# A third MLP pass moves to fifteen block products, with buffers and the instruction order rearranged to allow it

## The chip, the cores and the metric

The kernel runs on one core of a Trainium2 chip. The metric is the device time of one execution in microseconds (us). A core has five engines with an instruction queue each: PE (matrix products), DVE (vector), ACT (scalar functions and copies), POOL (vector work, slower) and SP (here it only issues transfers). Every engine runs its queue in order; an instruction that waits for a semaphore holds up all that stand behind it. Transfers (DMA) are issued from the queues of SP, ACT and POOL.

## The reference, cut to what matters

```python
# B, H, S, D = 4, 8, 768, 48; all float32; weights 384x1536 and 1536x384
k_n = k / (norm(k) + 1e-6)
for t in range(S):                      # a delta-rule recurrence per batch and head
    y[t]  = q[t] @ state
    v_old = k_n[t] @ state
    state = state + beta[t] * outer(k_n[t], v[t] - v_old)
x  = y as (B, S, H*D)                   # (4, 768, 384)
xn = (x - mean(x)) / sqrt(var(x) + 1e-6) * g_ln
out = x + maximum(xn @ w_ch1, 0) @ w_ch2
```

The weights arrive as 64-bit floats and are read as pairs of 32-bit words.

## The kernel before

**Chunks.** The sequence is cut into 12 chunks of 64 positions. All 32 recurrences (4 batches x 8 heads) run side by side. Within a chunk the recurrence is solved in closed form: the Gram matrix G of the chunk's keys, scaled by beta and the key norms, gives a unit triangular matrix whose inverse X turns values into updates u. With the state S before the chunk: u = X(v - K S), y = Q S + (masked Q K^T) u, and S grows by K^T u.

In the code: `products` builds G (`gram`, L834) and the query products (`queries`, L843); `recur(c)` (L1021) holds a chunk's steps: K S and Q S (L1033), u (L1088), the state's growth (L1105, read from raw keys in `kraws`), y (L1095), copies of y (L1133), layer norm (L1139 to L1155), and the turned, normalised activations `xnt` (by PE transposes for chunks 0 to 2, `LNPE`, by way of DRAM later).

**Inverses.** For chunk 0 `first_inverse` (L707) doubles the block size in five rounds; a round is a product E (L771), a predicated copy (DVE, L752 or L776), a product Z (L786), transposes (DVE, L735) and copies (ACT, L729). Ahead of it stand the transposes of raw keys (L628) and their copies out of PSUM (ACT, L633), the squares of the keys (ACT, L654), the norms' roots (ACT, L656) and G (L695, L743). For later chunks `rows_inverse` (L865) solves rows of blocks for many heads at once: 31 pairs of DVE instructions (L907, L914). Keys and queries come as blocks by `load_blocks` into a tile `tb[i]` and are turned there by DVE (`turned`, L799); key blocks alternate between `tb[0]` and `tb[2]`, issued on POOL's queue (L401).

**Weights.** Twelve pieces are fetched as words from ACT's queue (`fetch`) and turned into 32-bit floats by `convert`: ACT (L584, L592), DVE (L589), POOL (L602).

**MLP.** `mlp(c)` is one pass over the 256 rows of a chunk. In its plain form the first product takes 12 x 3 matmuls of 128x128 by 256 columns (L1407). From pass `FROM` on it runs as `fifteen(c)`: W1 and the activations are cut into 3x3 and 3x2 blocks, and 15 products of sums of blocks, each 4 matmuls of 128 columns (L1307), take the place of 18 block products. The sums of activations are made on POOL (`mix`, L1290), the results combined on ACT (L1325, L1334) and DVE (L1330), and the sums of W1 once, by `sums_of_w1` on POOL and DVE (L1265, L1267), half in place and half in new tiles. The second product is `seven(c)` from pass 1 on: 7 products instead of 8 (L1504), with combinations of hidden activations on POOL (L1491, L1529). Pass 0 uses the plain form (L1429).

**Order.** Every instruction group is a numbered step. `Line.emit` writes them out in the order of the string `ORDER`, which fixes each engine's queue; an assertion demands that a step's declared reads and writes (the key tuples) have gone before. The word `f` in `ORDER` puts in a filler: a product of zeros, 128x256, on PE (L1582). `due`, `cap`, `pr` and `t0` are arguments of the planner that made the string, and play no part when the program is built.

```python
FROM, LATER = 3, 6
kraws = [sb(f"kr{i}", [128, GH * DP]) for i in range(3)]
more = [t.rearrange("p h t -> p (h t)") for t in (qts[1], pts[1])] + [sb("w_more", [128, 2 * FB4])]
```

Of the kernel before, what the change touches and what calls it, by code (L numbers as in the profile page):

```python
# [16 lines left out]
C = 64  # L17
# [106 lines left out]
def act(n):  # L124
    return 0.17 + 0.83e-3 * n
# [6 lines left out]
47 9 6 257 8 48-49 10-11 13 1 32 26 23 14 0 12 65 7 66 60 39-43 256 45-46 44 61 55 74 53-54 52 58-59 327 56-57 63  # L132
405 408 64 37 21 5 17 30 71 35 73 69 75 238 79-80 82 85-86 96 89 88 36 29 15-16 20 4 18-19 90 33 97 87 91-92 3 93
98-99 83 100 94 84 101 81 106 104-105 103 76 38 27 95 102 124 22 125 118 126 239 119 24 77 108 70 107 109-110 215 78
226 127 111 122 121 112 129 72 246 123 240 128 213 133 25 134 120 f f 130 31 114 28 131-132 f f 135-137 141 115 2
142-143 222 139 138 140 147-150 216 145 230-231 146 144 157 151 116-117 214 159 153 152 158 209-210 163 250 154-155
161-162 160 156 211 164 113 401 403 314-316 412 260 325 67 313 326 265 410 259 262 68 264 263 266 261 413-414 328
407 409 212 f f 168 165 227 166-167 248 232 218 172-173 171 174 318 228 178 249 170 169 175-176 317 180-183 241 233
229 217 251 320 177 319 179 242 244 267 224 234 f 185 321 184 186 191 268-269 50 192 34 270-271 187 273 258 272 638
245 193 274-279 219 280 f f 197 243 322 370 329 323 188 195 330 189-190 331 194 196 247 369 332 363 650 652 399 199  # L140
198 200-201 205 333 204 364 202-203 206-207 334 208 335 f f f f 339 337 281-290 235 223 291-296 338 297-298 340 299
252 300-301 51 302-303 62 640 225 469 400 f 341-342 371 343-344 361-362 236-237 642 654 347 253 348 365 352 f f 435
434 402 324 404 336 411 304 474 477 406 476 475 307 305 767 309-310 312 308 311 306 437 436 345-346 353 372 349-351
354 220 373 367 221 374 f f f 438 355 359 439 360 366 440 415 357-358 356 478 577 575 254 578 581 479 368 255
480-482 418 416 473 484 643 641 637 644 656 649 655 639 653 768-769 771 773 772 770 766 419 576 375-376 579 614 420
580 583-584 379 377 582 388 381-382 421 485-503 422 504-509 378 510 423 511 645 587 615 585 616-617 387 588 591 424
586 592 428 427 426 595-596 425 417 380 651 589 429 441 599 618-619 442 774 512-523 394 430 433 431 590 383 432 393
443-444 385 389 445 593 524-526 390 657 527-528 448 446-447 384 529 600-602 646 908 449-450 391 397 395 1052 1054
1064 386 530 453 531 454 451-452 392 1066 603 647 604 658 620-621 594 458 455 605-606 597 607 659 456 532-533 459
534 460 457 461 465-466 464 467-468 463 462 598 622-623 608 396 535 483 398 1068 1065 536-539 629 540 630 541 631  # L150
542-543 632 544-547 633 609 778 775 805 624 610 625 806 910 912 763 907 911 764 914 901 648 913 660 909 900 662 1160
663-665 915 776 548 1056 1051 1057 1055 666 765 906 661 611 626 667-670 672 1162 550 549 551 903 552 628 627 673-674
902 905 1163 904 1165 1157 1167 613 811-812 807 777 809 817 810 818 675-677 815 808 816 823 821-822 824 813-814 1070
1069 829 832 830 833 1067 1053 678 779 679-690 553 691-701 554-558 838 819 702-704 634 705-706 564 707-711 559 827
839-840 562 561 560 563 828 820 780 841-842 848-849 843 781 712 1063 831 835 845 836 713 784 782 714 565 786 785 567
844 789 787 783 790 834 1058 825 850 715 788 568 826 794 791 566 569 795 716-717 796 792 718-719 793 720 855-856
851-852 865 916 853-854 801 797 570 866 846 873 867 837 802 799 804 574 572 571 800 573 803 798 917 721 1059 1526
847 1525 918 722-723 920 724 635 725-728 857 868 874-875 869 876 919 921 870 858 877 859-860 729-730 636 731-735
1347 1166 1348 1155-1156 1164 612 1168 736 1169 922-923 871 861 880-883 671 924 1071 1060 878-879 925 1061 1072
471-472 470 862 1528 1538 1170 1161 863-864 954 948 1073 927 891-893 956-957 884 894 872 926 895 962 896 1171 897  # L160
885 960 930-931 935 963 968 928 936 929 1540 1530 949 1075 951 950 739-740 1352 1062 1074 737-738 1077 1076
1078-1079 1172 886 969 961 932 937 741 1173 742 745-746 1080 958-959 743 974-975 744 887-888 955 980 953 933 952 752
# [78 lines left out]
2937-2938 2909 2939 2930 2940 2910 2964-2965 2954-2955 2941 2956 2942 2933 2957-2958 2966 2959 2943 2934 2967 2944  # L241
2960 2935 2968-2969 2971-2972 2945 2948 2946-2947 2970 2952 2951 2961 2981 2949-2950 2962 2953 2989 2982 2990-2992
2983 2963 2984 2993-2994 2973 2985-2986 2974-2976 2979-2980 2978 2995 2987 2996 2988 2997-3001 2977 3002 3007-3012
3003-3004 3013 3005 3014-3015 3006
"""


# [1482 lines left out]
```

## Time and profile before

| what | value |
|---|---|
| time, median of 3 runs | 529.24 us (527.1 to 530.44) |
| the profiled execution's own time | 530.82 us |
| its span, from first to last instruction | 529.1 us |
| PE busy | 496.1 us, 94% of the span |
| DVE busy | 358.6 us, 68% |
| POOL busy | 284.3 us, 54% |
| ACT busy | 207.2 us, 39% |
| first MLP product starts | 75.18 us |
| PE busy, 0 to 80 us | 58.0 us |

How to read the profile: all times are from one execution. A row of a timeline gives start, length, engine, line, output and inputs, shapes and count, and in brackets the idle time before it with what ended it. A float32 matmul leaves two records. Matmuls are pipelined, so the mean length of one record is longer than the step from one to the next; that step is what a product costs. "PEclk", the granted clock, is 1.00 at full speed. The chain that ended last is followed back from the last instruction, at each step to what released it.

### The profile page before, as it was taken

How to read it: one execution, taken by the hardware profiler on the slowest of the kernel's cores; microseconds unless marked ns; L12 is line 12 of the kernel's file. 1: busy time of each engine (PE TensorE's matmuls, PEld its weight loads, DVE VectorE, ACT ScalarE, POOL GpSimd, SP SyncE). 2: the span in 40 equal slices, each digit the busy share in tenths (PEclk: the TensorE clock that was granted, in tenths of full speed). 3: DMA queues.
4: the chain of work that ended last, by engine and by line, in shares of the span. 5: the costliest groups of instructions: out<-in, count | busy, mean ns of one | idle time of the engine just before them, and what ended most of it. 6: DMA issues, size and time to landing. Idle time of an engine off the chain costs nothing.

```text
span 529.1 us, 22717 instructions
## 1 busy us (share of the span) xinstructions
PE 496.1 (94%) x9938; PEld 451.6 (85%) x9938; DVE 358.6 (68%) x819; ACT 207.2 (39%) x451; POOL 284.3 (54%) x447
## 2 busy tenths in 40 slices
PE   5667988999999999989999999999999999999996
PEld 2455776767888889979999999999999999999996
DVE  2547778878997599986899954998837436354241
ACT  1786562542442334233261452353423424424130
POOL 7004485447245967767649437346374362554644
PEclk9588899999999999999999999999999999999999
DMA  9876759749543893159357267234343502102011
GB/s 178 200 161 122 211 89 233 118 121 164 101 69 81 178 156 55 35 147 191 60 120 135 48 184 126 45 85 75 97 100 71 117 4 60 34 33 59 1 32 30
DMA packets 181635, 54.56 MB, mean 103 GB/s; under 512 B 164888, under 2 KB 177312, under 8 KB 181536
## 3 DMA queue, kind: packets, MB, share of 16 engines
q1 hardware_dynamic: 168512, 40.10, 37.9%
q10 hardware_dynamic: 10816, 9.83, 6.7%
q0 software_dynamic: 2208, 3.17, 3.6%
q8 instruction: 78, 1.28, 1.0%
q14 instruction: 21, 0.17, 0.1%
HBM read 36.30 MB, written 16.78 MB: 100 GB/s over the span
## 4 chain that ended last, share of the span: by engine, by line
PE 85%; DVE 5%; issue 3%; DMA 2%; ACT 2%; SPq 1%; ACTq 0%; POOL 0%; DVEq 0%
PE f L1504 28%; PE f L1307 22%; PE f L1407 9%; PE two L819 3%; PE f L1429 3%; PE f L1582 2%; PE by L1033 2%; PE by L1095 2%; PE two L1088 2%; PE two L1033 2%; PE two L1105 2%; DVE xb L914 1%; DMA words<-in_moe_w_ch_dram 1%; SPq L401 1%; DMA kr<-in_k_dram 1%
## 5 line engine op out<-in xcount | busy, mean ns | idle before, releaser
L1504 PE MATMUL f<-w_sb,h_all 128*128 128x192 f32 x396 | 81.8, 329 | 0.0
L1491 POOL TENSOR_TENSOR h_all<-h_all 128x256 f32<-128x256 f32 x99 | 72.9, 753 | 14.9 <-DVE tmp L907 6.1
L1504 PE MATMUL f<-words,h_all 128*128 128x192 f32 x396 | 78.4, 330 | 0.1
L1330 DVE TENSOR_TENSOR h_all<-f,h_all 128x512 f32<-128x512 f32 x72 | 49.1, 686 | 33.3 <-PE f L1307 25.4
L1529 POOL TENSOR_TENSOR words<-h_all 128x128 f32<-128x128 f32 x66 | 31.2, 491 | 70.0 <-ACT h_all L1334 34.2
L1504 PEld LDWEIGHTS f<-w_sb,h_all 128*128 128x128 f32 x396 | 65.3, 190 | 1.1 <-POOL h_all L1491 0.2
L1504 PEld LDWEIGHTS f<-words,h_all 128*128 128x128 f32 x396 | 64.8, 190 | 1.4 <-issue 0.2
L914 DVE TENSOR_TENSOR xb<-xb,tmp 128x31 f32<-128x31 f32 (+19 forms) x139 | 58.8, 423 | 3.1
L907 DVE TENSOR_TENSOR tmp<-xb,gb 128x31 f32<-128x31 f32 (+19 forms) x139 | 53.0, 381 | 4.0 <-POOL xb L894 0.6
L1407 PE MATMUL f<-xnt,w_sb 128*128 128x256 f32 x216 | 52.6, 391 | 0.3 <-issue 0.3
L1325 ACT COPY h_all<-f 128x512 f32<-128x512 f32 x45 | 26.0, 586 | 58.8 <-PE f L1307 41.0
L401 POOL DMA_DIRECT2D tb<-in_k_dram x64 | 42.0, 660 | 13.0 <-DVE xb L914 7.4
L1334 ACT ACTIVATE h_all<-h_all 128x512 f32<-128x512 f32 x54 | 32.3, 625 | 36.2 <-DVE h_all L1330 36.0
L1407 PEld LDWEIGHTS f<-xnt,w_sb 128*128 128x128 f32 x216 | 40.4, 192 | 7.0 <-ACT h_all L1416 0.4
L1307 PE MATMUL f<-x_new,w_sb 128*128 128x128 f32 x288 | 39.8, 277 | 1.3 <-DVE h_all L1330 1.1
L1307 PE MATMUL f<-xnt,w_sb 128*128 128x128 f32 x288 | 40.7, 277 | 0.0
L1522 DVE TENSOR_TENSOR o<-f,x 128x192 f32<-128x192 f32 x33 | 11.6, 354 | 41.7 <-PE f L1504 24.9
L602 POOL TENSOR_TENSOR w_sb<-words 128x768 uint32<-128x768 uint32 (+1 forms) x11 | 15.0, 1365 | 43.3 <-DVE words L589 33.4
L1307 PEld LDWEIGHTS f<-x_new,w_sb 128*128 128x128 f32 x288 | 36.7, 192 | 1.7 <-issue 1.5
L1307 PEld LDWEIGHTS f<-xnt,w_sb 128*128 128x128 f32 x288 | 37.1, 191 | 0.3
L1133 ACT COPY x<-by 128x384 f32<-128x384 f32 x23 | 10.4, 481 | 53.2 <-POOL o L1522 36.3
L1416 ACT ACTIVATE h_all<-f 128x256 f32<-128x256 f32 x36 | 13.4, 383 | 35.1 <-PE f L1407 34.9
(252 smaller groups left out, 987.4 us busy)
## 6 DMA issues: line engine op xcount, KB each, us to landing
words<-in_moe_w_ch_dram ACTq DMA_DIRECT2D x20, 384.0 KB, 4.6
gd<-gsb SPq DMA_DIRECT2D x11, 512.0 KB, 3.9
v<-in_v_dram SPq DMA_DIRECT2D x24, 192.0 KB, 3.9
kr<-in_k_dram SPq DMA_DIRECT2D x46, 96.0 KB, 3.6
out_dram<-o SPq DMA_DIRECT2D x46, 96.0 KB, 2.3
xld<-xlt SPq DMA_DIRECT2D x9, 384.0 KB, 2.5
xnt<-xld SPq DMA_DIRECT2D x36, 96.0 KB, 3.0
tb<-in_q_dram SPq DMA_DIRECT2D x40, 64.0 KB, 2.9
```

The source lines that it names most:

```text
L401: add(eng, cost, lambda: QUEUE[eng].dma_start(out=out_, in_=in_), r, w, bulk=n * ns / 16e3, np=n, **kw)
L907: lambda j=j, n=n, w=w, t=t: nc.vector.tensor_tensor(out=t, in0=xv[:, 0:n, j : j + 1].to_broadcast([128, n, w]), in1=gv[:, j : j + 1, j + ...
L914: "DVE", dve(n * w), lambda t=t, rest=rest: nc.vector.tensor_tensor(out=rest, in0=rest, in1=t, op=ALU.subtract),
L1033: nc.tensor.matmul(dst[half(e), hp, j], src[drows(hp), (e if n else key_half(c, hp, e)) * GP + j], s_all[drows(hp), e, j], start=(n == 0 o ...
L1307: nc.tensor.matmul(wide(p[:, f : f + 128]), w[:, f : f + 128], r, start=start and i == 0, stop=True, skip_group_check=True)
L1325: add("ACT", act(512), lambda: nc.scalar.copy(o, p), pk, ok)
L1330: add("DVE", dve(512), lambda: nc.vector.tensor_tensor(out=o, in0=x, in1=y, op=op), [*xk_, *yk], ok)
L1334: add("ACT", act(512), lambda: nc.scalar.activation(o, o, ACTF.Relu, scale=scale), [], ok)
L1407: nc.tensor.matmul(p[:, 0:TOK], w1_sb[:, t, f * 128 : (f + 1) * 128], xnt[:, t], start=(t == 0), stop=(t == KC - 1))
L1491: add(eng, cost, lambda: e.tensor_tensor(out=out_, in0=x, in1=y, op=op), r, w, port=2 if eng == "Pool" else 1, pr=-2)
L1504: lambda f=f, t=start and f == order[0]: nc.tensor.matmul(p[:, 0:D2], lhs(f), rhs[:, f], start=t, stop=(f == order[-1]), skip_group_check=True
L1529: lambda f=f + i: e.tensor_tensor(out=s3[f], in0=one(0, 0)[0](f), in1=one(1, 0)[0](f), op=ALU.subtract),
```

## The change

`FROM` goes from 3 to 2, so the pass of chunk 2, until now plain, uses the fifteen products; 10 of 12 passes do. Its activations lie in another order (`LNPE`), so `fifteen` takes a second view for them. W1's sums must be ready a pass earlier, while the second tiles for q and P are still in use; they get two tiles of their own and `tb[2]`. To make room, raw keys have two buffers instead of three, and from chunk 4 on all key blocks go through `tb[0]`. Chunks 2 and 3 load raw keys into `tb[0]` and `tb[2]`.

Besides, a tiny square root of one column moves to the front of ACT's work (a key "act" makes copies and conversions follow it), `convert` of half a piece counts both halves' transfers as read, POOL's clearing of all of `tb[0]` becomes DVE's clearing of its padding, and the whole `ORDER` is new, with 30 fillers in place of 19.

```diff
-    FROM, LATER = 3, 6
+    FROM, LATER = 2, 6
...
-    kraws = [sb(f"kr{i}", [128, GH * DP]) for i in range(3)]
+    kraws = [sb(f"kr{i}", [128, GH * DP]) for i in range(2)]
...
-    more = [t.rearrange("p h t -> p (h t)") for t in (qts[1], pts[1])] + [sb("w_more", [128, 2 * FB4])]
+    more = [sb(f"w_more{i}", [128, 2 * FB4]) for i in range(2)] + [tb[2]]
...
-    for i in (2, 1):
+    for i in (2, 1, 0):
         c_dve(
             lambda i=i: nc.vector.memset(tb[i].rearrange("p (h d) -> p h d", d=DP)[:, :, D:], 0.0), 0.28, [("tbpad", i)],
         )
+    c_dve(lambda: nc.vector.memset(eps, 1e-6), 0.06, ["eps"])
+    add("ACT", 1.48, lambda: nc.scalar.sqrt(rstd[:, 0, 0:1], eps), ["eps"], [("ln", 0, 0), "act"], t0=2.2)
...
-    c_dve(lambda: nc.vector.memset(eps, 1e-6), 0.06, ["eps"])
-    add("ACT", 1.5, lambda: nc.scalar.sqrt(rstd[:, 0, 0:1], eps), ["eps"], [("ln", 0, 0)], t0=2.2)
...
-        wk = WORD_KEYS[BUF[i]] + [("wd", BUF[i], c0 // 384 + y) for y in range(n // 384)]
+        wk = WORD_KEYS[BUF[i]] + [("wd", BUF[i], y) for y in range(2)] + ["act"]
...
-        gone = GONE + [("gb2", n) for n in range(4)] + ["xb2"]
+        gone = [("tb", 2, e, hp) for hp in range(2) for e in range(2)] + [("tbpad", 2)]
...
-            return xnt[:, k].rearrange("p (i g b) -> p g i b", g=2, b=BK)[:, 1 - t], [*xk(k), ("xb", c % 2, k, t)]
+            v = xnt[:, k].rearrange("p (g i b) -> p g i b", g=2, b=BK) if c <= LNPE else xnt[:, k].rearrange("p (i g b) -> p g i b", g=2, b=BK)
+            return v[:, 1 - t], [*xk(k), ("xb", c % 2, k, t)]
...
-    c_pool(lambda: nc.gpsimd.memset(tb[0], 0.0), 1.0, [("tbpad", 0)], t0=30.0)
...
-            if c == 2:
-                load_raw(c, pr=pr, t0=27.0)
-                first_kt(kraws[2], raw_keys(2), *kt, PAIRS[3], pr=pr, t0=40.0)
-            elif c == 3:
-                keys = [("tb", 2, e, hp) for hp in range(2) for e in range(2)]
-                load_raw(c, dst=tb[2], keys=keys, pr=pr, t0=29.0)
-                first_kt(tb[2], keys + [("tbpad", 2)], *kt, PAIRS[3], pr=pr, t0=40.0)
+            if c < 4:
+                i = 2 * (c % 2)
+                keys = [("tb", i, e, hp) for hp in range(2) for e in range(2)]
+                load_raw(c, dst=tb[i], keys=keys, pr=pr, t0=27.0)
+                first_kt(tb[i], keys + [("tbpad", i)], *kt, PAIRS[3], pr=pr, t0=40.0)
             else:
-                load_blocks(2 * (c % 2), k, c, "Pool", pr=pr, t0={2: 80.0, 3: 120.0}.get(m, 40.0 * m - 20))
-                turned(c, 2 * (c % 2), *kt, pr=pr)
+                load_blocks(0, k, c, "Pool", pr=pr, t0={2: 80.0, 3: 120.0}.get(m, 40.0 * m - 20))
+                turned(c, 0, *kt, pr=pr)
```

The first steps that the two orders put on ACT's queue, up to the roots of chunk 0's norms ("wd" is a transfer of weights):

```
before: key transfer, wd, key transfer, table load, eye copy, wd, eye copy, wd, wd, wd,
        conversion (L584), squares, squares, key copy, eye copy, key copy, table load, roots
after:  key transfer, key transfer, table load, tiny root, eye copy, eye copy, squares, wd, key copy,
        wd, wd, eye copy, squares, key copy, wd, wd, roots
```

## The prediction

> **What bounds the kernel now.** I read the page first: busy shares, slices of the span, the chain that ended last.
>
> ```profile
> span 529.1 us, 22717 instructions
> PE 496.1 (94%) x9938; PEld 451.6 (85%) x9938; DVE 358.6 (68%) x819; ACT 207.2 (39%) x451; POOL 284.3 (54%) x447
> ...
> PE   5667988999999999989999999999999999999996
> ...
> PE 85%; DVE 5%; issue 3%; DMA 2%; ACT 2%; SPq 1%; ACTq 0%; POOL 0%; DVEq 0%
> ```
>
> PE is busy 496.1 of 529.1 us, and the 33 us in which it is not lie mostly in the first seven slices of 13.2 us. There are thus two regimes. From the first MLP product (75.18 us) on, PE is the bound and time is PE work plus a few stalls. Before that, a chain of dependent steps of chunk 0 sets the pace: raw keys, their norms, the Gram matrices, five rounds of the inverse, u, y, layer norm. What is cut from that chain shifts everything behind it. So I took the timelines of ACT and PE for the start.
>
> ```profile
> 9.76 1.09 PE L628 MATMUL by<-ident,kr 128*128 128x128 f32 x8
> 17.87 1.13 PE L695 MATMUL by<-kt 48*64 48x64 f32 x32 [5.72 <-ACT kt L633]
> 23.40 1.13 PE L771 MATMUL two<-qt,gsb 64*64 64x64 f32 x32 [0.45 <-DVE qt L758]
> 24.46 2.07 PE L1582 MATMUL f<-u 128*128 128x256 f32 x4
> 60.50 2.01 PE L1582 MATMUL f<-u 128*128 128x256 f32 x8
> 75.18 4.12 PE L1407 MATMUL f<-xnt,w_sb 128*128 128x256 f32 x18 [0.28 <-issue]
> ```
> ```profile
> 14.98 0.54 ACT L584 ACTIVATE words<-words 128x384 f32<-128x384 f32 x1 [5.46 <-DMA words<-in_moe_w_ch_dram]
> 15.43 0.92 ACT L654 ACTIVATE xln<-kr 128x384 f32<-128x384 f32 x2
> 17.84 1.28 ACT L656 ACT_TABLE_LOAD   x1
> ```
>
> PE has the keys of chunk 0 turned from 9.76 us on, but the copy out of PSUM stands on ACT behind a conversion of weights (L584), and that waits 5.46 us for a weight transfer. PE idles 5.72 us over it. Then ACT loads a second function table, 1.28 us, before the square roots of the norms. The inverse's first product is at 23.40 us.
>
> For the price of an MLP product, two long pieces of the chain in which PE runs one line without a break:
>
> ```profile
> 131.70 7.97 PE f L1407 x36
> ...
> 473.11 9.82 PE f L1307 x88
> ```
>
> A record of the plain product (256 columns) takes 7.97/36 = 0.2214 us; one of the fifteen-product form (128 columns) 9.82/88 = 0.1116 us. The granted clock stands at 1.00 in both.
>
> **The change, part by part.**
>
> (1) *Third pass in fifteen products.* A plain pass has 216/3 = 72 records of L1407. A fifteen-product pass has 15 products of 4 tiles, 60 matmuls, two records each: 120. So 72 x 0.2214 = 15.94 us become 120 x 0.1116 = 13.39 us: **-2.55 us** of PE, in the regime where PE is the bound.
>
> What it adds elsewhere: ten sums on DVE (L1330, 90 in nine passes, 0.686 us) 6.9 us; twelve mixes on Pool (L1290, about 0.46 us) 5.5 us; on ACT five copies of 0.586 and six rectifications of 0.625 instead of twelve of 0.383, 6.7 against 4.6 us. All of it runs beside MLP products on PE. The tightest cover is DVE's: it is busy 36.09 of 40 us from 200 to 240 us, where PE shows 2.85 us of idle time. If the sums stood wholly in the way of the recurrence there, they would cost 6.9 us; nothing if PE always has products to run. PE's rows name DVE for little (1.1 us before L1307 in all), so I am near the lower end: **+0.5 us** (0 to 6.9).
>
> (2) *W1's sums earlier.* The same 14 on Pool (1.26 to 1.72 us) and 2 on DVE, into tb[2] and two tiles of their own instead of the second buffers of q and P. They move from 172 to 229 us to between the start of the first MLP and the third pass, in Pool's queue among weight conversions and key blocks. Pool is busy 41 of the 80 us from 60 to 140, so 20 us fit; the work that hides it is MLP products of passes 0 and 1. I take 0; the first of them stands ahead of weight conversions that the first MLP needs, so one or two of 1.27 us could show: 0 to +2.5.
>
> (3) *Key blocks through one tile, raw keys in two buffers.* Chunk 2m+1's eight transfers on Pool's queue may now start only after DVE has turned chunk 2m's (L799, 1.23 us); behind them in that queue stand the combinations for the second product (L1491), for which PE's weight loads wait. Pool idles 13.0 us before these transfers already, 7.4 of it for DVE, and PE waits 0.2 us for L1491. Raw keys land some 3.6 us after issue and now wait, on SP, for the state update two chunks back, not three, with most of a pass of some 40 us left; behind them stand v and q of the same chunk. Both 0; a single bad wait of Pool's kind costs up to the 7.4 us seen.
>
> (4) *The start, order anew.* On ACT the new order is: two key transfers, one table load with the square root in it, the eye copies, the squares, and only then weight transfers; the first conversion comes after the first round of the inverse. I walk it with the durations of this trace. Let the keys land at 8.47 us as now (3.22 + 5.25 in the chain). Square 0.50, transfer 0.38, copy of keys 0.57, two transfers 1.05, eye copy 0.61, square 0.50, copy 0.57: 12.65. Then PE: Gram 0.6, four transposes 0.6, beta 0.3, second Gram 1.1 (half clock): 15.25. DVE: scale 0.69, predicated copy 0.74, norms of the other half 0.6, scale 0.68, transpose 0.70: 18.7. With small waits the first inverse product stands at about 19.2 instead of 23.40: -4.2 us. The keys may land earlier, since no weight transfer is issued between theirs.
>
> Not all of this need reach the first MLP. Ahead of the copies of y the new order has two more 384-column and two more 768-column scalings (2 x 0.57 + 2 x 0.92 = 3.0 us) and a root on ACT, and a 1.23 us transpose and two shifts (0.31 + 0.55) on DVE. ACT's cover is its idle time in the chain, 3.0 us before 43.47 and 3.6 before 56.97. Bounds: 0 if the extra work eats it all; -7.3 if the 5.46 us wait, its 0.54 us conversion and the 1.28 us table load all come off. I take **-4.0 us**, near the walk.
>
> [...]
>
> (5) *Fillers.* The new order has 30 filler products (L1582) where the old has 19, all before the first MLP. A filler is two records: 1.03 us in the row at 24.46, where the clock is 0.50, and 0.50 us in the row at 60.50, where it is 1.00. Placed where PE waits they cost nothing, and they keep the clock up. Eleven more cost 0 to 11.3 us; I take 0, since a round lasts 7 to 8.7 us (from the first product of one to that of the next) while PE has about 4 us of work in it (four products of 0.65, a Gram of 1.1, transposes of 0.6).
>
> [...]
>
> **The sum.** -2.55 + 0.5 - 4.0 = -6.05 us. The profiled execution took 530.82 us (span 529.1 and 1.7 around it): 524.8. The median shown is 529.24, 1.6 below that execution; from it, **523.2 us**, 1.1% faster. A difference of 1% (5.3 us) is about what a measurement of this kernel can tell from no change.
>
> **The rivals.**
>
> *A. The start's gain is eaten before the first MLP.* ACT carries conversions, key copies and the copies of the inverse in one queue; if the extra 3.2 us fall between two rounds, they come off the 4.0, with the DVE transpose ahead of the layer norm (1.2 us) the rest. Left: -2.55 + 0.5, 527.2. For it: ACT is busy 15.59 of 20 us from 20 to 40. Against: 11.19 of 20 from 40 to 60.
>
> *B. Fillers at half clock: slower.* Place: PE's queue between the first inverse product and the first MLP. If the clock falls there, a filler takes 1.03 us and stands ahead of a product that is ready; a row of six of them then lasts 6.2 us, more than the rest of a round. It decides once PE reaches them late and cold. Price: 11 x 1.03 = 11.3 us, the start's gain gone with it: 529.24 - 2.55 + 0.5 + 11.3 = 538.5. For it: the row at 24.46 and one at 53.11 (2.07 us for two) did this. Against: fewer idle gaps ahead of them now.
>
> *C. The start gains its upper bound or more.* Keys land earlier and PE keeps full clock in round 1, where it has 0.50 now (a product 1.13 instead of 0.65 us): -2.55 + 0.5 - 8.7 (7.3 and three products at 0.48 less) = 518.5.
>
> *D. Fifteen products bring no PE time.* If each needed its operands from DVE and Pool just in time, 2.55 us would turn into waits and about 6.9 us of sums would show: with the start's -4.0, 529.24 + 6.9 - 4.0 = 532.1, unchanged. Against: nine passes show 1.1 us of such waits.
>
> **How the numbers follow.** Forecast 0.50, its own range 518.5 to 527; A 0.18; B 0.15; C 0.12; D 0.05. Faster by over 1% (below 523.9): 0.8 of the forecast and all of C, 0.40 + 0.12 = 0.52, and 0.02 of A where the eating stops short: 0.54. Slower by over 1% (above 534.5): B, 0.02 of D, and 0.02 of the forecast, should a wait like that of part (3) come more than once: 0.19. Within: the rest, 0.27. Range 515 to 536: it holds the forecast, A, C and D and the lower part of B.
>
> **What would show it.** Right: ACT's first squares by 9 us, no wait for weights before them, one table load; the first inverse product near 19 us, the first MLP product near 71 instead of 75.2; 144 records of L1407's line and 1200 of L1307's. Wrong: fillers over 0.6 us each on the chain (B); the first inverse product early but the first MLP product still near 75 (A); PE idle above 6 us between 100 and 250 us (D, or part 3).

## The result: about 1% slower, and the start's gain is gone before the first MLP product

| kernel | median of 20 runs | profiled execution | its span | first inverse product | first MLP product | from there to the end |
|---|---|---|---|---|---|---|
| before | 528.57 us (525.33 to 536.14) | 530.82 us | 529.1 us | 23.40 us | 75.18 us | 453.9 us |
| after | 534.03 us (529.47 to 538.06) | 530.97 us | 529.3 us | 17.40 us | 75.52 us | 453.8 us |

The ratio of after to before is 1.0096, with a 95% interval of 1.0069 to 1.0123; it leaves out the slowest runs (one of before, two of after), which lie over 1.5% above the fastest of their kernel. The forecast was 523.2 us. The table says at once where to look: the first inverse product comes 6.0 us earlier, and the first MLP product does not. The profiled execution of after is 3.1 us under its median, so part of the slowdown is in no row below.

The page of the changed kernel, cut to the parts shown of before (span and busy time; PE by slices; the chain that ended last, by engine):

```profile
span 529.3 us, 22938 instructions
PE 498.1 (94%) x10008; PEld 452.4 (85%) x10008; DVE 359.3 (68%) x829; ACT 208.1 (39%) x449; POOL 289.1 (55%) x457
...
PE   6768789899989999999999999999999999999996
...
PE 75%; DVE 8%; SPq 6%; DMA 4%; issue 3%; ACT 2%; POOL 1%; ACTq 0%; DVEq 0%; POOLq 0%
```

PE is busy 2.0 us more than before. Its first slices are fuller (67687898 against 56679889), but with other work: fillers. PE's share of the last chain falls from 85 to 75%.

The timeline of ACT: the table load at 2.27 us, the first squares at 6.67 us, and a copy that waits 6.99 us for fillers.

```profile
2.27 1.28 ACT L422 ACT_TABLE_LOAD   x1 [2.27 <-issue]
6.67 0.51 ACT L657 ACTIVATE xln<-kr 128x384 f32<-128x384 f32 x1
...
55.11 0.37 ACT L732 COPY xt<-f 128x256 f32<-128x256 f32 x1 [6.99 <-PE f L1586]
```

The timeline of PE over the same stretch (lines moved by three or four: L774 was L771, L1586 was L1582, L1411 was L1407):

```profile
17.40 0.69 PE L774 MATMUL two<-qt,gsb 64*64 64x64 f32 x32 [0.34 <-DVE qt L761]
...
27.90 0.70 PE L1586 MATMUL f<-u 128*128 128x256 f32 x2 [2.20 <-ACT xt L732]
...
32.90 1.45 PE L631 MATMUL f<-ident,tb 128*128 128x128 f32 x8 [2.06 <-DMA tb<-in_k_dram]
...
50.53 4.54 PE L1586 MATMUL f<-u 128*128 128x256 f32 x12
55.00 0.69 PE L774 MATMUL two<-qt,gsb 64*64 64x64 f32 x32
58.32 0.69 PE L774 MATMUL by<-qt,gsb 64*64 64x64 f32 x32 [2.63 <-ACT xt L732]
...
75.52 4.52 PE L1411 MATMUL f<-xnt,w_sb 128*128 128x256 f32 x18
```

A first inverse product as early as this one should bring the fifth round forward too. It starts at 55.00 us (before: 55.12 us), behind a row of twelve records, six fillers, that takes 4.54 us, most of it at half clock (0.51 from 51 to 54 us). The last transpose that this product needs ends at 52.31 us, so the fillers put it off by 2.7 us (DVE's timeline):

```profile
51.88 0.43 DVE L738 STREAM_TRANSPOSE qt<-by 128x256 f32<-128x256 f32 x1
```

Its second product then waits 2.63 us for ACT: the copy it needs is one that ACT does late, because ACT stood 6.99 us before the copy shown above.

### The profile page after: what moved, and what is told of

It reads as the page before. It is cut to its first block, busy times and chain, and to the rows that moved or that the text cites. A ratio compares the mean times of both kernels' runs of the same rounds, so it can differ in the third digit from the quotient of the medians.

```text
span 529.3 us, 22938 instructions
## 1 busy us (share of the span) xinstructions
PE 498.1 (94%) x10008; PEld 452.4 (85%) x10008; DVE 359.3 (68%) x829; ACT 208.1 (39%) x449; POOL 289.1 (55%) x457
## 4 chain that ended last, share of the span: by engine, by line
PE 75%; DVE 8%; SPq 6%; DMA 4%; issue 3%; ACT 2%; POOL 1%; ACTq 0%; DVEq 0%; POOLq 0%
PE f L1508 26%; PE f L1311 23%; SPq L404 6%; PE f L1411 5%; PE f L1433 3%; PE two L822 3%; PE by L1036 2%; PE by L1098 2%; PE two L1091 2%; PE two L1108 2%; PE two L1036 2%; PE f L1586 1%; DMA words<-in_moe_w_ch_dram 1%; DVE xb L917 1%; DVE tmp L910 1%
## 5 line engine op out<-in xcount | busy, mean ns | idle before, releaser
L1334 DVE TENSOR_TENSOR h_all<-f,h_all 128x512 f32<-128x512 f32 x80 | 54.2, 685 | 23.2 <-PE f L1311 18.9
L917 DVE TENSOR_TENSOR xb<-xb,tmp 128x31 f32<-128x31 f32 (+19 forms) x139 | 54.0, 388 | 2.8
L910 DVE TENSOR_TENSOR tmp<-xb,gb 128x31 f32<-128x31 f32 (+19 forms) x139 | 52.9, 381 | 3.3 <-POOL xb L897 0.4
L1338 ACT ACTIVATE h_all<-h_all 128x512 f32<-128x512 f32 x60 | 36.1, 625 | 30.6 <-DVE h_all L1334 30.5
L1311 PE MATMUL f<-xnt,w_sb 128*128 128x128 f32 x320 | 44.8, 278 | 0.7 <-issue 0.7
L1311 PE MATMUL f<-x_new,w_sb 128*128 128x128 f32 x320 | 44.5, 277 | 0.1
L1311 PEld LDWEIGHTS f<-xnt,w_sb 128*128 128x128 f32 x320 | 40.5, 192 | 1.4 <-issue 0.9
L1311 PEld LDWEIGHTS f<-x_new,w_sb 128*128 128x128 f32 x320 | 40.6, 192 | 0.7 <-issue 0.3
L1411 PE MATMUL f<-xnt,w_sb 128*128 128x256 f32 x144 | 34.7, 387 | 0.1
L1411 PEld LDWEIGHTS f<-xnt,w_sb 128*128 128x128 f32 x144 | 26.4, 190 | 4.7 <-ACT h_all L1420 0.5
L1508 PE MATMUL f<-w_sb,words 128*128 128x192 f32 x132 | 27.0, 328 | 0.0
L1311 PE MATMUL f<-xnt,tb 128*128 128x128 f32 x160 | 22.9, 279 | 1.3 <-issue 0.7
```

The lines of the kernel that those rows point to most:

```text
L910: lambda j=j, n=n, w=w, t=t: nc.vector.tensor_tensor(out=t, in0=xv[:, 0:n, j : j + 1].to_broadcast([128, n, w]), in1=gv[:, j : j + 1, j + ...
L917: "DVE", dve(n * w), lambda t=t, rest=rest: nc.vector.tensor_tensor(out=rest, in0=rest, in1=t, op=ALU.subtract),
L1311: nc.tensor.matmul(wide(p[:, f : f + 128]), w[:, f : f + 128], r, start=start and i == 0, stop=True, skip_group_check=True)
L1334: add("DVE", dve(512), lambda: nc.vector.tensor_tensor(out=o, in0=x, in1=y, op=op), [*xk_, *yk], ok)
L1338: add("ACT", act(512), lambda: nc.scalar.activation(o, o, ACTF.Relu, scale=scale), [], ok)
L1411: nc.tensor.matmul(p[:, 0:TOK], w1_sb[:, t, f * 128 : (f + 1) * 128], xnt[:, t], start=(t == 0), stop=(t == KC - 1))
```

## The experiments

Three theories were put against each other for the lost 6 us. **T1**: the six fillers ahead of the fifth round, with the ACT copy behind them. **T2**: SP's queue, on which 14.83 us of query transfers stand ahead of the keys of chunk 2 that PE waits for at 32.90 us. **T3**: weight conversions on ACT that now stand between the copies of round two. A number in a diff below is a numbered step in `ORDER`; 197 and 199 are the fifth round's two products. "f" is a filler. Each ratio is taken to runs of the kernel before beside them on the same chip; in brackets stands its 95% interval, and the time given is the median.

**The changed kernel again (again).** 

> The changed kernel as it is, beside the others of this group, for a second profile of it. Its first profile (530.97 us) has the first MLP product at 75.5 us and 454 us from there to the end; the median of 20 runs is 534.0. If the missing 3 us are the start's, the first MLP product stands near 78 here; if they lie behind it, it stands near 75.5 again, and the stretch to the end takes 457 us or more, at a lower granted clock. Time against the kernel before: 1.007 to 1.012.

It took 530.19 us against 527.06, ratio 1.0059 (1.0026 to 1.0091): slower, by less than at first. The first inverse product is at 17.38 us.

```profile
50.01 2.88 PE L1586 MATMUL f<-u 128*128 128x256 f32 x12
52.82 0.70 PE L774 MATMUL two<-qt,gsb 64*64 64x64 f32 x32
56.12 0.69 PE L774 MATMUL by<-qt,gsb 64*64 64x64 f32 x32 [2.60 <-ACT xt L732]
74.29 4.15 PE L1411 MATMUL f<-xnt,w_sb 128*128 128x256 f32 x18
```

Here the same six fillers run at full clock in 2.88 us. The last transpose ends at 51.73 us, so they put the fifth round off by 1.1 us instead of 2.7, and the wait for ACT stands as it was, 2.60 us. One row of fillers thus varies by 1.7 us from run to run.

**Without the six fillers (no_six).**

```diff
- ... 297 298 f f f f f f 197 299 300 301 ...
+ ... 297 298 197 299 300 301 ...
```

> The changed kernel without the row of six fillers ahead of the fifth round's products. Theory 1 (fillers stand on the inverse's chain): the fifth round's first product starts when the last transpose is done, 52.4 instead of 55.0 us, the second right behind it, 53 instead of 58.3, because the copy out of the bank that the fillers write no longer waits for them; first MLP product at 70 to 72 instead of 75.5, time 4 to 5 us under the changed kernel: 529 to 530, ratio 0.999 to 1.002. Theory 2 (waits in SP's and ACT's queues set the rounds): the first MLP product stays within 1 us of 75.5, ratio 1.007 to 1.012. Clock rival: without the six the granted clock falls below 0.7 from 53 to 62 us and the later products take 1.1 us; first MLP product at 74 to 76.

Ratio 1.0004 (0.9975 to 1.0033), 527.28 us: six fillers fewer, and the kernel is level with before and 2.9 us under again (530.19).

```profile
54.02 1.13 PE L774 MATMUL two<-qt,gsb 64*64 64x64 f32 x32 [1.32 <-DVE qt L738]
55.68 1.13 PE L774 MATMUL by<-qt,gsb 64*64 64x64 f32 x32 [0.52 <-ACT xt L732]
73.50 4.15 PE L1411 MATMUL f<-xnt,w_sb 128*128 128x256 f32 x18
```

The wait for ACT falls from 2.63 to 0.52 us. The profiled execution had a bad start (first inverse product at 19.91 us, 2.5 us later, at a granted clock of 0.50 from 9 to 18 us), and still its first MLP product is 2.0 us ahead of after's. The product now starts when the last transpose is done (53.97 us). T1 holds for these six.

**Without any filler (no_fill).** All 30 are taken out. 

> The changed kernel without any of its 30 fillers. Theory 1: every round gets shorter, the first MLP product at 67 to 71 us, time 526 to 530, ratio 0.995 to 1.002. Clock rival: with PE idle between products the granted clock stays near 0.5 from 17 to 60 us, some 20 products of the rounds take 1.1 instead of 0.69 us (9 us), first MLP product at 77 or later, ratio 1.012 or more. Theory 2: 73 to 76, ratio 1.005 to 1.012.

Ratio 1.0094 (1.0061 to 1.0127), 532.76 us: no better than after. The windows (length; busy time of PE, PEld, DVE, ACT and POOL, with counts; granted clock; DMA share; GB/s), first of after, then of this kernel:

```profile
20.00:40.00 20.00, 14.27 (x411) 10.96 (x409) 13.02 (x34) 14.83 (x33) 7.12 (x10) 0.91 0.76 158
```
```profile
20.00:40.00 20.00, 14.39 (x401) 12.68 (x400) 10.65 (x29) 13.28 (x31) 5.47 (x7) 0.69 0.61 128
```

The granted clock falls from 0.91 to 0.69, and the first MLP product is at 76.64 us. So the other 24 fillers earn their place: without them too the kernel is 5.5 us over no_six. It was these six, where they stood, that cost more than they brought.

**Chunk 2's keys ahead of chunk 1's queries on SP (query_later).**

```diff
- 141 143 408 113 ... 324 413
+ 141 143 113 ... 324 408 413
```

> The changed kernel with one transfer moved: the first half of chunk 1's queries, which holds SP's queue from 6.3 to 21.1 us, goes behind the raw keys of chunks 2 and 3. Theory 2 (this wait makes chunk 2's raw keys late, and their transposes stand ahead of the third round on PE): those transposes no longer wait 2.06 us, the third round's first product starts at 31 instead of 34.3, the first MLP product at 72 to 73.5, ratio 1.003 to 1.006. Theory 1 (the six fillers set the end of the rounds): the third round starts earlier, but the fifth still waits for fillers; first MLP product at 74 to 75.5, ratio 1.007 to 1.010.

Ratio 1.0063 (1.0024 to 1.0102), 530.64 us, against 1.0059 for after beside it (again).

```profile
33.51 1.97 PE L631 MATMUL f<-ident,tb 128*128 128x128 f32 x8
35.41 0.69 PE L774 MATMUL by<-qt,gsb 64*64 64x64 f32 x32
```

The 2.06 us wait for keys is gone from the row of L631, but the third round's product still comes at 35.41 us (after: 34.28 us). The clock is down there (0.54 from 28 to 35 us), so the row alone does not settle it, but again, which has such a fall (products of 1.08 to 1.14 us between 29 and 33 us), has this product at 33.97 us, and the runs gain nothing. T2 falls.

**Conversions behind the copies of round two (act_first).** 248, 226 and 250 are the conversions on ACT, 249 one on DVE; 149 is the round's second product.

```diff
- ... 248 27 249 24 147 139 226 145 140 250 144 146 f 149 212 148 150 227
+ ... 27 24 147 139 145 140 144 146 248 226 250 f 149 212 148 150 249 227
```

> The changed kernel with one thing moved: in the second round, three conversions of weights on ACT (0.9, 0.56 and 0.9 us) and one DVE step that follows them go behind the six copies of the inverse instead of between them. Theory 3 (copies that stand behind conversions on ACT hold the rounds): the second round's second product starts at 26 to 26.5 instead of 28.5 to 29.0 us; but the fifth round still waits for the row of six fillers, so of the 2 to 2.5 us between 1 and 2.5 reach the first MLP product, 72.5 to 74; ratio 1.002 to 1.006. Theory 1 alone: the rounds behind absorb it, first MLP product at 74 to 75.5, ratio 1.006 to 1.010.

Ratio 1.0042 (1.001 to 1.0074), 529.52 us. From the inverse's first product (round one) to round two's second product it is 10.36 us, against 11.13 and 11.64 us in the two profiles of after: 0.8 to 1.3 us, instead of the 2 us and more expected.

```profile
28.03 0.70 PE L1586 MATMUL f<-u 128*128 128x256 f32 x2 [1.42 <-ACT xt L732]
28.66 0.69 PE L774 MATMUL by<-qt,gsb 64*64 64x64 f32 x32
```

PE's wait for ACT's copies ahead of that product falls from 2.20 us (after) to 1.42 us, and this rest stays with no conversion between the copies. T3 is true and small.

**Copies ahead of the six fillers (six_behind).** To tell PE's delay from ACT's, ten ACT steps were moved in the written order to stand before the six fillers. Every engine's queue is as in after; only what waits for what changes (the copies no longer wait for the fillers, the fillers wait for one copy). A filler writes columns 256 to 511 of `f_[0]`; the late copy reads columns 0 to 255 of the same bank, and in after, where it is written behind the fillers, it waited 6.99 us for them.

```diff
- ... f f f f f f 197 ... 194 333 334 412 414 196 372 190 222 195 ...
+ ... 194 333 334 412 414 196 372 190 222 195 f f f f f f 197 ...
```

> The changed kernel with the same instructions in the same order on every engine; only in the order in which the groups are written out, the row of six fillers stands behind ACT's copies of round four instead of ahead of them. So ACT no longer waits for the fillers, the fillers wait for one copy of ACT. It splits theory 1 in two. If the wait of the copies is the dearer half: the fifth round's second product follows the first at once instead of 3.3 us later, first MLP product 2 to 3 us earlier, 72 to 73.5, ratio 1.002 to 1.005. If the fillers' own time on PE is (2.9 to 4.5 us): the first product of the round stays at 53 to 55 us, the first MLP product within 1 us of 75, ratio 1.006 to 1.010.

Ratio 1.0033 (1.0007 to 1.0058), 527.59 us.

```profile
52.00 2.88 PE L1586 MATMUL f<-u 128*128 128x256 f32 x12
54.81 0.69 PE L774 MATMUL two<-qt,gsb 64*64 64x64 f32 x32
55.86 0.69 PE L774 MATMUL by<-qt,gsb 64*64 64x64 f32 x32 [0.36 <-ACT xt L732]
...
72.86 4.23 PE L1411 MATMUL f<-xnt,w_sb 128*128 128x256 f32 x18
```

The fillers are still there, and the wait for ACT falls to 0.36 us. So the six cost twice: on PE, ahead of a ready product, and on ACT, by holding a copy that has nothing to do with them. The measured order, after 1.0059 and 1.0096, this 1.0033, no_six 1.0004, fits a share for each, though the intervals of neighbours overlap: the rows show the split, the times do not.

No run here lets a filler and the copy meet in the bank, so whether the wait on a filler in its other half is needed was not shown. As the program stands the wait is there and took 6.99 us, so a filler belongs in a bank that no copy is about to read.

**Plain third pass in the changed program (from3, from3_spread).** The new order and buffers stay; the third pass goes back to plain products, and eight sums of W1 move to its end and behind it, in a row or one by one.

```diff
-    FROM, LATER = 2, 6
+    FROM, LATER = 3, 6
```

> The changed kernel with the third pass in plain form again (FROM = 3), all else as in the changed kernel: buffers, start, fillers; six of the sums of W1 then stand between the third pass and the fourth. If the fifteen products bring PE time as predicted (2.55 us, less up to 0.5), this is 2 us slower than the changed kernel: 533 to 536, ratio to before 1.009 to 1.013. Theory 4 (the fifteen products bring nothing in their place, since the sums and mixes cost what PE saves, or a record costs more there than 0.1116 us): same time as the changed kernel or up to 1 us less, ratio 1.004 to 1.008.

> As the run before with the third pass in plain form, but the eight sums of W1 that must wait for this pass stand one by one between the other work of Pool, right behind the pass's last first-stage product, where five stood in a row (6.8 us) and PE waited 2.75 us. What the fifteen products are worth in this place: if 2.05 us as predicted, this kernel is 2 us slower than the changed kernel, ratio to before 1.011 to 1.017 (the changed kernel had 1.0096 and 1.0059). If a record of them costs 0.1225 us there, as the rows of the changed kernel's profiles from 150 to 200 us say, and a plain one 0.223 (the second profile of before), 120 x 0.1225 against 72 x 0.223 is 1.4 us, and the changed kernel idles 1 to 2 us more from 120 to 200 us: 0 to 1 us in all, ratio 1.006 to 1.011. If the changed third pass costs more than it brings: 1.000 to 1.005.

Ratios 1.0246 (1.0207 to 1.0284) and 1.0232 (1.0186 to 1.0279). One line of PE's timeline from each, then the sums on POOL in from3 (line numbers are a little lower here):

```profile
221.32 0.71 PE L1309 MATMUL f<-x_new,w_sb 128*128 128x128 f32 x4 [2.75 <-POOL w_sb L1268]
```
```profile
217.79 1.46 PE L1506 MATMUL f<-words,h_all 128*128 128x192 f32 x4 [3.08 <-POOL h_all L1493]
```
```profile
218.44 6.84 POOL L1268 TENSOR_TENSOR w_sb<-w_sb 128x512 f32<-128x512 f32 x5
```

The sums placed after the third pass make PE wait for POOL, whichever way they are strung: idle time after the first MLP product is 11.1 and 11.0 us, against 7.7 and 6.6 in after. The third pass itself takes 16.53 us of plain products in both, against 14.60 in after. From the first MLP product to the end it is 465.5 and 460.2 us against 453.8. Of these 11.7 and 6.4 us, idle time makes 3.4 and 3.3, the third pass 1.9 each. Much of what is left in from3 is the clock: it is 0.50 from 100 to 106 us, from 161 to 164 and from 223 to 225 (from3_spread: from 218 to 221), where after has 1.00, and by the clock alone PE can lose up to half of these 11 and 3 us, an estimate. So undoing the fifteen products costs more than it gives back in this program. But these runs do not price them alone, since the sums lose their hiding place with them, and the clock falls where after's profile has no fall.

**Putting the findings together (tuned), and further down the chain (tuned2, tuned3, tuned4, ln_first).** tuned is no_six and act_first, with round four's predicated copies and transposes on DVE ahead of parts of the first chunk inverse, and with the transposes of chunk 2's keys (316, 317) behind the third round's first product, in place of the three fillers there (`f f f 165` becomes `316 317 637 639 638 636 165`).

> The changed kernel with four moves together: the row of six fillers out, the three fillers ahead of the third round's second product out, the transposes of chunk 2's keys there instead of ahead of the third round; ACT's copies of the second round ahead of conversions; DVE's steps of the first chunk inverse behind the transposes of rounds four and five. Theories 1 and 3: each round 7 us or less, first MLP product at 66 to 69 us, time 521 to 525, ratio 0.988 to 0.995. Theory 2 or a clock that falls for want of fillers: first MLP product not under 72, ratio 0.998 to 1.004.

Ratio 0.9981 (0.9955 to 1.0006), 526.77 us: the best of all, and not to be told from before.

```profile
50.97 0.69 PE L774 MATMUL two<-qt,gsb 64*64 64x64 f32 x32 [0.16 <-DVE qt L738]
55.08 1.13 PE L774 MATMUL by<-qt,gsb 64*64 64x64 f32 x32 [3.41 <-ACT xt L732]
```

The fifth round starts 4 us ahead of after's, the first MLP product 3.0 (72.49 us). The four transposes ahead of it take 1.4 us from first to last (49.48 to 50.92), where they take 4.1 in after. The four kernels that follow try to carry this to the MLP. tuned2 and tuned3 move ACT's five copies of Grams and weights behind round four's last copy, and other DVE work back; tuned4 does the same with the first chunk inverse (287 to 301) behind the fifth round (200), and a block transpose on DVE (644, L802) with a load behind the layer norm (350). The list has the main moves; tuned2 also brings more inverse steps (156, 164 to 176) ahead of other work. ln_first is after with the last move of tuned4 alone.

```diff
+ tuned2: tuned; 333 334 414 372 222 behind 195; two fillers out; 350 behind 353; 354 behind 358
+ tuned3: tuned; 333 334 414 372 222 behind 195; 287-301 behind 200; 350 behind 353; 354 behind 358
+ tuned4: tuned; 333 334 414 372 222 behind 195; 287-301 behind 200; 644 648 behind 350
+ ln_first: after; 644 648 behind 350
```

> The kernel with the four moves (0.998 of before), with more of the same kind: in rounds three and five ACT's copies of the inverse ahead of conversions and of chunk 3's Gram copies (the fifth round's second product waited 3.41 us for them), in rounds three and four DVE's predicated copies and transposes ahead of the first chunk inverse, two of four fillers out ahead of round four, layer norm's second half ahead of chunk inverse and second product of queries. Theories 1 and 3 (what stands ahead of the inverse in a queue sets the start): first MLP product at 64 to 68 instead of 72.5 us, time 518 to 523, ratio 0.981 to 0.991. Rival (PE is behind by then with work that has to be done anyway, or the clock falls): first MLP product under 70 but time 525 or more, ratio 0.994 to 1.000.

> The kernel with the four moves (ratio 0.998), and of the second set only what its trace asked for: in round five ACT's copies and DVE's predicated copies go ahead of Gram copies and of the first chunk inverse; layer norm's second half ahead of the next chunk's inverse; and one sum of weights on Pool (1.6 us) ahead of the clearing that waits for that inverse, since PE waited 3.22 us for it in the second set. Theories 1 and 3: fifth round done by 54 us, first MLP product at 67 to 70.5, no wait for weights over 1 us behind it, time 519 to 524, ratio 0.984 to 0.994. Rival (weights bound the first MLP pass from then on): first MLP product under 71, but waits for weights or for ACT take 2 us or more right behind it; ratio 0.995 to 1.000.

> The changed kernel with one DVE step moved: the transpose of chunk 4's key blocks (1.25 us, L802) stands behind both halves of the first layer norm instead of ahead of it; one transfer on Pool that waits for it moves along. If DVE's queue in front of layer norm sets the first MLP product, that comes 1.2 us earlier, 73 to 74.5, ratio to before 1.004 to 1.008 (the changed kernel: 1.0096 and 1.0059). If weights set it, it stays at 74.3 to 75.5 and a wait for weights shows ahead of the first pass; ratio 1.006 to 1.010.

> The kernel with the four moves (0.998), with round five's copies and predicated copies ahead of Gram copies and of the first chunk inverse (as in the third set), and the transpose of key blocks behind layer norm; layer norm, the next chunk inverse and the sums of weights otherwise as in the kernel with the four moves. If DVE's queue ahead of layer norm is what kept the gain: first MLP product at 68.5 to 71 us, time 522 to 525, ratio 0.990 to 0.996. If weights or something else behind it: first MLP product at 72 or later, or waits of 2 us or more in the first pass; ratio 0.997 to 1.003.

None brought the gain hoped for: 1.0072 (1.0038 to 1.0106) for tuned2, 1.0072 (1.0045 to 1.01) for tuned3, 1.0122 (1.0072 to 1.0173) for ln_first and 1.0015 (0.9981 to 1.0049) for tuned4, which came out as its rival said. tuned4 has the fifth round's second product at 52.52 us, 5.8 us ahead of after's, and its first MLP product at 73.08 us: 3.4 of the 5.8 us are lost in the 20.6 us between (after: 17.2 us). The windows from 47 to 73 us, of after and of tuned4, then the row on which PE waits longest there:

```profile
47.00:73.00 26.00, 20.16 (x523) 16.12 (x522) 15.51 (x44) 13.46 (x29) 11.74 (x13) 0.93 0.57 127
```
```profile
47.00:73.00 26.00, 19.58 (x674) 15.64 (x674) 21.75 (x53) 15.94 (x35) 14.51 (x17) 0.99 0.72 176
```
```profile
71.84 1.30 PE L1036 MATMUL two<-s_all,kt 48*64 48x48 f32 x64 [2.16 <-DVE pt L853]
```

DVE is busy 21.75 of 26 us instead of 15.51, and PE waits 2.16 us for its product with `pmask` (L853) and 1.22 for the layer norm, where after waits 0.93 and 0.60. The first chunk inverse, the shifts, the transpose and the layer norm all stand in one queue, and what goes first makes the others late. In ln_first the moved transpose stands ahead of the product with `pmask` and of the activations (DVE's timeline), and the first MLP product slips to 78.38 us. Not all of that need be the move's: this profile has a granted clock of 0.50 from 59 to 65 us.

```profile
73.76 1.24 DVE L802 STREAM_TRANSPOSE kt<-tb 128x1024 f32<-128x1024 f32 x1
...
76.03 1.22 DVE L853 TENSOR_TENSOR pt<-two,pmask 128x1024 f32<-128x1024 f32 x1
77.16 0.55 DVE L1192 TENSOR_TENSOR xnt<-by,g_sb 128x384 f32<-128x384 f32 x1
```

tuned2 gets it to 70.94 us, the earliest of all, and then waits 3.22 us for its weights:

```profile
70.94 0.66 PE L1410 MATMUL f<-xnt,w_sb 128*128 128x256 f32 x2
74.81 1.13 PE L1410 MATMUL f<-xnt,w_sb 128*128 128x256 f32 x4 [3.22 <-POOL w_sb L604]
```

So three things stand close behind one another here: the rounds, DVE's queue and the weights. Where one was shortened, the next showed.

**The kernel before, again (before_again).** To see the scatter. 

> The kernel before, unchanged, for a second profile of it. Its first profile (530.82 us, 2 us over its median) has 453.9 us from the first MLP product to the end, as the changed kernel's profiles have (453.8 and 455.9); the prediction took 2.05 us off for the fifteen products. Theory 4 (the fifteen products bring less than 2.05 us in place): this stretch is 453 to 454 us again. Rival (the first profile of before was a long one there, and the kernel before is simply quicker behind 75 us): 450 to 452 us.

It took 527.24 us. First inverse product 23.31 us, fifth round 53.25, first MLP product 73.32, from there to the end 452.2. So the way from the first inverse product to the first MLP product varies by 1.8 us (51.8 and 50.0) with nothing changed, and every profile is read against a band of that width.

## Why the prediction was wrong, point by point

**Step 4, the start: the walk was right, the "-4.0" failed.** The walk gave the first inverse product at 19.2 us and 4.2 us gained; it came at 17.40 and 17.38, 6.0 us gained; the squares start at 6.67 us where the walk let the keys land at 8.47, the same 1.8 us. No conversion waits ahead of the squares, and there is one table load. But the step took "-4.0, near the walk" to the first MLP product, and there the two profiles of after have 75.52 and 74.29, of before 75.18 and 73.32: nothing. Its lower end, "0 if the extra work eats it all", was what happened, though not by the scalings it named: those that act_first moved are worth 0.8 to 1.3 us. The walk went along the chain only as far as the first product, and not through the five rounds behind it. Where the 6.0 us went, by the first product of each round (us; means of two profiles each):

| | round 1 | round 2 | round 3 | round 4 | round 5 | first MLP product |
|---|---|---|---|---|---|---|
| before | 23.4 | 31.0 | 39.1 | 45.5 | 54.2 | 74.2 |
| after | 17.4 | 25.0 | 34.1 | 44.1 | 53.9 | 74.9 |
| lead of after | 6.0 | 6.0 | 5.0 | 1.4 | 0.3 | -0.7 |

More than half of it, 3.6 us, goes in round three, before the six fillers. DVE's timelines of after, then of before, from the end of that round:

```profile
39.47 1.40 DVE L910 TENSOR_TENSOR tmp<-xb,gb 128x15 f32<-128x15 f32 x1
40.79 0.43 DVE L738 STREAM_TRANSPOSE qt<-two 128x256 f32<-128x256 f32 x1
...
43.38 0.44 DVE L738 STREAM_TRANSPOSE qt<-by 128x256 f32<-128x256 f32 x1
```
```profile
45.07 0.78 DVE L735 STREAM_TRANSPOSE qt<-two 128x256 f32<-128x256 f32 x2
45.90 0.78 DVE L735 STREAM_TRANSPOSE qt<-by 128x256 f32<-128x256 f32 x2
```

In after the first chunk inverse (L910) starts ahead of the transposes that round four waits for, and its next steps stand between them: the four transposes take 3.0 us from first to last (again: 2.7). In before they take 1.6; there the chunk inverse starts at 53.25 us, behind the transposes for round five. The prediction counted a transpose and two shifts as DVE's extra work and not these steps. No run moves these steps alone in round three, so this part is read from rows and not tested.

**Step 5, the fillers: "I take 0" failed.** Most of them earn their place (no_fill). The argument, a round of 7 to 8.7 us with 4 us of PE work, is an average, and the six stand where that slack had been used up: they put a ready product off by 2.7 or 1.1 us on PE, and the next by 2.1 to 2.3 us on ACT by way of the PSUM bank (2.63 and 2.60 us of wait against 0.52 and 0.36). The prediction had looked at PE alone; a wait on another engine for a filler's bank does not occur in it.

**Step 1, fifteen products: right sign, "-2.55" mis-sized, and not seen in the total.** To measure it, PE's first-product records of one pass are added from the start of each to the start of the next record on PE, without idle time. The third pass takes 16.04 us in both profiles of before (15.94 forecast) and 14.60 and 14.61 in those of after (13.39 forecast): 1.4 us saved, and the term that was mis-sized is the price of a fifteen-product record, 0.122 us here. The 0.1116 us came from the last pass, which is the cheapest: the nine passes of before go from 14.24 us (0.119 a record) down to 13.41. The fourth pass, the nearest, would have given 1.7 us. Single rows say less; PE's timeline of after has eight records in 0.99 us in the third pass, and the same late in the kernel:

```profile
185.02 1.16 PE L1311 MATMUL f<-xnt,w_more 128*128 128x128 f32 x8
186.01 1.06 PE L1311 MATMUL f<-x_new,w_sb 128*128 128x128 f32 x8
...
475.70 1.16 PE L1311 MATMUL f<-x_new,w_more 128*128 128x128 f32 x8
476.69 1.50 PE L1311 MATMUL f<-xnt,w_sb 128*128 128x128 f32 x12
```

What makes a record dearer among other work stays open.

**"+0.5" for the sums on DVE** does not show as a wait for them: ahead of the fifteen products PE waits 0.6 us for DVE's sums in both profiles of after, 1.1 us in both of before. All its idle time after the first MLP product is 7.7 and 6.6 us against 6.8 and 5.4, some 1 us more. In sum the second half does not move. From the first MLP product to the end, eight profiles that have after's order from there on, or nearly so, have 450.3 to 455.9 us, mean 453.2, and the last four variants (tuned2, tuned3, tuned4, ln_first) 455.1 to 457.0; before has 453.9 and 452.2. The -2.05 of step 1 with its sums is not visible in that scatter, part of which is the clock: again has a granted clock of 0.72 between 96 and 108 us (1.00 in after, 0.86 in both profiles of before), which makes some 3.4 us, an estimate from 12 x 0.28.

**Steps 2 and 3, W1's sums and the buffers: "0" was right.** In after PE waits nowhere for the sums, and its idle time between 100 and 250 us is 4.4 us (before: 4.5), below the 6 us named as a sign against. The sums run from 61 to 190 us, the last two inside the third pass, which starts at 175.9 us. POOL's idle time ahead of the key blocks' transfers, which step 3 feared, fell from 13.0 to 2.9 us. from3 shows that the sums' early place is no matter of course: placed later they cost 2.75 us in one wait.

**The rivals.** The signs on record for A came true (first inverse product early, first MLP product near 75), but not its price: 527.2 us is 3.0 us under again's median and 6.8 under the first one. The causes it named were not the main ones either: ACT's scalings are a small part (act_first), and moving the DVE transpose behind the layer norm gained nothing (ln_first). Other DVE steps between the rounds, and B's place, "a row of six" fillers ahead of a product that is ready, took the gain. B's price, 11 x 1.03 us, was too high: taking out six won 2.9 us, and taking out all won nothing. Its sign, fillers at over 0.6 us each, showed, but it could not decide. The groups of PE's lines in after, then in before (busy us, mean ns, idle before):

```profile
L1586 PE MATMUL f<-u 128*128 128x256 f32 x60 | 18.7, 446 | 2.8 <-ACT xt L732 2.2 <-DVE qt L738 0.6
```
```profile
L1582 PE MATMUL f<-u 128*128 128x256 f32 x38 | 13.8, 493 | 4.1 <-DVE qt L735 2.7 <-DVE u L1074 0.8 <-issue 0.5
```

30 fillers take 18.7 us, 0.62 each; the 19 of before took 13.8, 0.73 each. A and B stood as rivals, and each held a part. C fell with the first MLP product. D fell with the 1.4 us of the third pass and the idle time between 100 and 250 us.

**In sum.** Predicted -6.05 us. By the means of two profiles each, the start gives +0.7 (74.9 against 74.25) and the rest +1.8 (454.9 against 453.05): 2.5 us slower, where runs give 3.1 (again) and 5.5 (after's first 20, 534.03 - 528.57). What stays open: the medians of the unchanged after, 534.03 and 530.19, lie 3.8 us apart while before's lie 1.5 apart, and no profile shows where that is. The clock is a part: the mean granted clock is 0.981 over the first 20 runs and 0.985 over again's 10, and within the 20 a clock lower by 0.01 goes with some 3 us more, so about 1 us (an estimate from these runs). Open too is what the fifteen products would bring with the start of before: no run has that.

## What to carry to other kernels

A gain at the head of a chain is worth what the next queues let through: walk it through every round to the point where the bound changes, on all engines, and name which queue (here DVE's, then the weights) stands just behind. Afterwards compare the lead round by round: it says where a gain is lost, which one late row does not. Place a filler by the slack of that one place, not of an average round, and count as its cost also who waits for the PSUM bank it writes (here ACT, 6.99 us). Take the price of a matmul from the pass nearest to the one that changes; here the last pass was the cheapest, and the third cost 9% more than it.

## What was not expected of the hardware

**A scaling on DVE ends just behind POOL's clearing.** In the layer norm the same scaling takes 1.26 us once and 0.47 us right after. DVE's and POOL's timelines of after:

```profile
69.55 1.26 DVE L1154 TENSOR_SCALAR xln<-x,mv,rstd 128x384 f32<-128x384 f32 x1
...
71.65 0.47 DVE L1154 TENSOR_SCALAR xln<-x,mv,rstd 128x384 f32<-128x384 f32 x1
```
```profile
68.23 1.48 POOL L605 TENSOR_TENSOR w_sb<-words 128x768 uint32<-128x768 uint32 x1
69.63 0.96 POOL L1638 MEMSET xt<- 128x1024 f32 x1
```

The long one ends at 70.81, 0.22 us behind POOL's clearing (70.59). In tuned and tuned4 it takes 1.68 and 1.88 us in one place and again ends 0.22 and 0.21 us behind the clearing (67.78 and 67.56; 67.07 and 66.86). In all three POOL is in a conversion (L605) when DVE's record starts; the short one of after, at 71.65 us, runs while POOL has no record (70.59 to 73.31 us). No run here took the clearing away, so the cause is not shown.

**The clock falls behind a short gap in some runs and not in others.** In after the granted clock is 0.51 from 51 to 54 us, where PE had idled 0.45 and 1.19 us just before, and with it the six fillers take 4.54 us; in again, with a gap of 1.25 us in the same place, it stays at 1.00 and they take 2.88. In ln_first, with a gap of 1.46 us there, they take 4.55 us, in six_behind, with one of 2.01 us, 2.88 us (clock 1.00 from 40 to 60 us). In before, clocks of 0.65 (40 to 44 us) and 0.63 (52 to 56 us) stand behind gaps of 2.60 and 2.67 us. So the length of the gap just before does not tell these cases apart, and what sets the fall is not shown.
